# Attention and MLP kernel on one core: every engine in written order, k summed ahead of its product, v pooled by halving adds

## The chip, the cores and the metric

The kernel runs on one core of a Trainium2 chip. The metric is the device time of one launch in microseconds (us); the kernel before takes 438.38 us (median of 3 runs, 438.37 to 439.07). Engines: PE (TensorE, matrix products), DVE (VectorE), ACT (ScalarE), POOL (GpSimd) and SP (SyncE, which here only issues DMAs).

## The reference

Two layers follow each other for 8 batches of 576 tokens and 8 heads of width 64. First an attention whose keys and values are means over 8 tokens (72 of each per head), then a mixing of tokens and a two-layer MLP (512 to 2048 to 512):

```python
k_p = k.reshape(B, H, 72, 8, D).mean(axis=3); v_p = v.reshape(B, H, 72, 8, D).mean(axis=3)
attn = softmax(q @ k_p.T / 8);  x = (attn @ v_p), heads side by side      # B, 576, 512
u = x + lam * einsum('ts,bsd->btd', w_tok, alpha1 * x + beta1)
out = u + lam * (relu((alpha2 * u + beta2) @ w_ch1) @ w_ch2)
```

## The kernel before, in words

Heads are taken in pairs (hp 0 to 3). For a batch b and a pair, `load_qk` (L72) loads q and k as 128 partitions of four tokens each, and the last 64 tokens by further DMAs; `load_v` (L94) loads v, 72 groups of 8 tokens. All these DMAs are issued by SP. `cast_qk` (L84) makes bf16 of q and k, four instructions a pair, on POOL in the main loop. `att_F` (L227) transposes q on PE (L233, L235), copies it to `qT` (L240, ACT), pools k by four products with a 0/1 matrix and one for the last 64 tokens (L245, L247), and casts the result to `kpT` (L249, L250, DVE). `att_V` (L252) pools v on DVE: one reduction over 8 tokens for each head (L256). `att_S` (L260) makes scores and their exponentials (ACT, L269) of one head; `att_AV` (L273) the product with v, whose quotient goes to x (DVE, L288, L290). `att_X` (L293) makes xs, the scaled x, for a range of heads (DVE, L297, L301). `mix_T` (L317) is the token mixing of one chunk of 128 tokens: five products on PE (L324), then u and u_bf on DVE (L327, L329). `mix_uT` (L332) transposes u_bf on PE (L340) and copies it by ACT (L342). Four chunks make a block of 512 tokens; there are 9 blocks. `mlp_A` (L348) is the first layer for one of 16 slices (four products, L351; ReLU by ACT, L354), `mlp_B` (L359) a quarter of the second layer for one of four chunks (L364), whose last quarter ends with an add on DVE (L369) and a store by SP.

The loop at L434 writes block n's 16 `mlp_A` and 16 `mlp_B` together with the attention of batch n+1 and the loads of batch n+2. Each step has a due time, in units of one `mlp_A`, and they are written in the order of due times: `att_F` of pair hp at 1.5 + 3.5 hp, `att_V` at 2 + 3.5 hp, the scores from 14.5, `att_AV` from 16.6, `att_X` at 20.7, 22.7 and 24.7, `mix_T` from 26, `mix_uT` from 27.8. Block 0 also holds three `setup_bias` (L217, PE) and four `scale_w2` (L210, DVE, due 8.2, 10.2, 12.2, 14.2). Blocks 7 and 8 have no attention.

Written order is not what runs: the framework orders each engine's instructions itself, by its own estimate of when each is ready, and an engine then runs its list strictly in order. Ahead of the loop, L378 to L410 write batch 0's attention, the load of the weights w1 and w2 (POOL's DMAs, cast on the way), the transposes of w_tok (`setup_wtok`, L172), the loads of batch 1 and the first four `mix_T`.

Of the kernel before, what the change touches and what calls it, by code (L numbers as in the profile page):

```python
# [23 lines left out]
def kernel(  # L24
# [98 lines left out]

    def bcast(src, name):
        t = const.tile([P, DM], FP, tag=name, name=name)
        nc.scalar.dma_start(out=t, in_=src.unsqueeze(0).to_broadcast((P, DM)))
        return t

    lam_bc = bcast(moe_lam, "lam_bc")
    al1_bc = bcast(moe_alpha1, "al1_bc")  # L130
    b1_bc = bcast(moe_beta1, "b1_bc")
    al2_bc = bcast(moe_alpha2, "al2_bc")
    b2col = const.tile([P, 4], FP, tag="b2col", name="b2col")
    nc.scalar.dma_start(out=b2col, in_=moe_beta2.rearrange("(c p) -> p c", p=P))


# [350 lines left out]
```

## Time and profile before

| | us |
|---|---|
| median of 3 runs | 438.38 |
| the profiled execution | 437.62 |
| its span on the core | 435.9 |
| PE busy / DVE busy / ACT busy / POOL busy | 370.4 / 233.2 / 181.8 / 71.9 |
| first product of the MLP (block 0 begins) | 64.46 |
| last add | 430.94 to 431.63 |

In the rows further down a timeline line gives start, duration, engine, line, operation, output and inputs, their shape and the count, and in brackets the idle time ahead of it with what ended that. A product's duration includes its way through the array, so that the distance of two starts, not the duration, is its cost. PEclk is the granted share of PE's clock.

### The profile page before, as it was taken

What the parts mean: (1) busy time and instruction counts of PE and PEld (TensorE: products, weight loads), DVE (VectorE), ACT (ScalarE), POOL (GpSimd) and SP (SyncE); (2) the same over time, 40 slices, a digit from 0 to 9 for tenths busy, and PEclk for the clock granted to TensorE, in tenths of its full rate; (3) what the DMA queues carried; (4) which work ended last, traced back from release to release, by engine and by line L of the source; (5) the groups of instructions that cost most, each with busy time, mean ns of one, the idle gap of its engine ahead of it and who ended that gap; (6) DMA issues with size and microseconds to landing.
All of it is one profiled execution on the core that took longest, in us unless ns stands there. A gap on an engine that the chain in (4) does not pass through costs nothing.

```text
span 435.9 us, 6112 instructions
## 1 busy us (share of the span) xinstructions
PE 370.4 (85%) x2315; PEld 191.5 (44%) x2358; DVE 233.2 (53%) x484; ACT 181.8 (42%) x348; POOL 71.9 (17%) x139
## 2 busy tenths in 40 slices
PE   0266529997899899978998999789989999999995
PEld 0145214553455345534553455345534554444442
DVE  3688479299318941894179417950696158301011
ACT  1133115741575057504760576047604771560720
POOL 2541629600140014001400140002000000000000
...
GB/s 206 227 257 224 251 210 131 227 226 134 43 145 132 104 50 141 130 104 25 164 117 117 28 110 76 102 28 2 16 59 24 2 26 48 26 0 72 26 24 72
DMA packets 43436, 44.71 MB, mean 103 GB/s; under 512 B 12624, under 2 KB 33104, under 8 KB 43408
## 3 DMA queue, kind: packets, MB, share of 16 engines
...
q10 hardware_dynamic: 1104, 1.05, 0.9%
q8 instruction: 18, 0.29, 0.3%
q14 instruction: 10, 0.08, 0.1%
...
## 4 chain that ended last, share of the span: by engine, by line
PE 55%; DVE 29%; DMA 12%; issue 2%; SPq 1%; ACT 0%
PE ps_h L351 29%; PE ps_ch L364 11%; DVE vp L256 10%; PE ps_tok L324 6%; DMA qk_raw<-in_q_dram 6%; DVE x_tm L290 5%; DVE xs L297 4%; DVE u_sb L369 4%; DMA v_hp<-in_v_dram 3%; PE ps_uT L340 2%; DMA b2col<-in_moe_beta_dram 2%; DVE u_sb L327 2%; DVE u_bf L329 2%; DVE rec L288 1%; PE ps_q L233 1%
## 5 line engine op out<-in xcount | busy, mean ns | idle before, releaser
L364 PE MATMUL ps_ch<-w,Hj 128*128 128x512 bf16 x553 | 136.5, 379 | 1.7 <-issue 0.6
L351 PE MATMUL ps_h<-u_fm,w 128*128 128x512 bf16 x557 | 132.1, 381 | 1.8 <-ACT u_fm L342 0.7
L354 ACT ACTIVATE Hj<-ps_h,bias_cols 128x512 bf16<-128x512 f32 x144 | 98.9, 687 | 57.0 <-PE ps_h L351 54.0
L351 PEld LDWEIGHTS <-w 128*128 128x128 bf16 x576 | 53.7, 98 | 59.9 <-issue 1.8
L89 POOL CAST qk_bf<-qk_raw 128x512 bf16<-128x512 f32 x60 | 42.5, 709 | 224.3 <-issue 153.4
L342 ACT COPY u_fm<-ps_uT 128x512 bf16<-128x512 bf16 x36 | 21.1, 585 | 130.8 <-PE ps_uT L340 130.8
L364 PEld LDWEIGHTS <-Hj 128*128 128x128 bf16 x576 | 51.8, 98 | 52.0 <-issue 1.6
L256 DVE TENSOR_REDUCE vp<-v_hp 72x64 f16<-72x512 f32 x64 | 63.3, 1002 | 7.4 <-DMA v_hp<-in_v_dram 7.2
L324 PE MATMUL ps_tok<-xs,wtT 128*128 128x512 bf16 (+2 forms) x199 | 50.6, 391 | 10.4 <-DVE xs L297 10.2
L269 ACT ACTIVATE ET<-ps_sc 72x288 f16<-72x288 f32 x128 | 43.9, 407 | 31.6 <-PE ps_sc L267 31.4
L369 DVE TENSOR_TENSOR u_sb<-u_sb,ps_ch 128x512 f32<-128x512 f32 x36 | 24.5, 681 | 51.4 <-PE ps_ch L364 48.3
L249 DVE CAST kpT<-ps_kp 64x72 bf16<-64x72 f32 x32 | 7.1, 223 | 81.0 <-PE ps_kp L247 80.9
L267 PE MATMUL ps_sc<-qT,kpT 128*72 128x288 bf16 x128 | 27.6, 307 | 9.7 <-DVE kpT L249 9.7
L327 DVE TENSOR_TENSOR u_sb<-x_tm,ps_tok 128x512 f32<-128x512 f32 (+1 forms) x40 | 26.8, 681 | 14.4 <-PE ps_tok L324 14.4
L324 PEld LDWEIGHTS <-wtT 128*128 128x128 bf16 (+3 forms) x200 | 19.2, 103 | 33.7 <-issue 17.6
L340 PE MATMUL ps_uT<-identity_bf,u_bf 128*128 128x128 bf16 x144 | 14.6, 226 | 20.7 <-DVE u_bf L329 20.7
L290 DVE TENSOR_TENSOR x_tm<-ps_av,rec 128x320 f32<-128x320 f32 x64 | 29.9, 480 | 0.3
L329 DVE TENSOR_TENSOR u_bf<-u_sb,al_bc 128x512 bf16<-128x512 f32 (+1 forms) x40 | 27.7, 705 | 0.8
L288 DVE RECIPROCAL rec<-ps_av 128x5 f32<-128x5 f32 x64 | 11.1, 182 | 30.4 <-PE ps_av L286 30.2
L91 POOL CAST qk_bf<-qk_raw 64x128 bf16<-64x128 f32 x60 | 25.7, 429 | 2.2 <-DMA qk_raw<-in_k_dram 1.8
L267 PEld LDWEIGHTS <-kpT 128*72 128x72 bf16 x128 | 14.9, 119 | 22.9 <-DVE kpT L249 10.0
L340 PEld LDWEIGHTS <-u_bf 128*128 128x128 bf16 x144 | 9.5, 99 | 33.1 <-DVE u_bf L329 29.8
...
## 6 DMA issues: line engine op xcount, KB each, us to landing
...
```

The lines of the kernel that those rows point to most:

```text
L89: eng.tensor_copy(out=bf[:, i, 0:4].rearrange("p c h d -> p h c d"), in_=raw[:, i, :, 0:4, :])
L256: nc.vector.tensor_reduce(out=vp1_pool[hp][:, hh, 0:64], in_=v_hp[:, hh].rearrange("g p d -> g d p"), axis=AX.X, op=ALU.add)
L267: nc.tensor.matmul(out=ps_sc[0:SPG, 0:288], lhsT=kpT_pool[hp][:, hh, :], rhs=st["qT"][hp][:, n0:n0 + 288])
L269: nc.scalar.activation(out=ET[:, n0:n0 + 288], in_=ps_sc[0:SPG, 0:288], func=AF.Exp, bias=0.0, scale=0.125)
L290: nc.vector.tensor_tensor(out=x[:, :, dd:dd + D], in0=av[:, :, 0:64], in1=rec.unsqueeze(2).to_broadcast((P, 5, D)), op=ALU.mult)
L324: nc.tensor.matmul(out=ps_tok[p0:p1, 0:DM], lhsT=wtT[0:kk, at, P * c:P * c + (p1 - p0)], rhs=xs[0:kk, sc, :], start=(sc == 0), stop=(sc == 4))
L327: nc.vector.tensor_tensor(out=s["u"][p0:p1, :], in0=st1[b]["x"][p0:p1, c, :], in1=ps_tok[p0:p1, 0:DM], op=ALU.add)
L329: nc.vector.tensor_tensor(out=s["u_bf"][p0:p1, :], in0=s["u"][p0:p1, :], in1=al2_bc[p0:p1, :], op=ALU.mult)
L351: nc.tensor.matmul(out=ps_h, lhsT=w1[:, cc, P * j:P * j + P], rhs=u_fm[n][:, cc, :], start=(cc == 0), stop=(cc == 3))
L354: nc.scalar.activation(out=t, in_=ps_h, func=AF.Relu, bias=bias_cols[:, j:j + 1], scale=1.0)
L364: nc.tensor.matmul(out=ps, lhsT=Hj[n, j][:, 128 * m:128 * m + 128], rhs=w2[:, j, :], start=(j == 0), stop=(j == NJ - 1))
L369: nc.vector.tensor_tensor(out=u, in0=u, in1=ps, op=ALU.add)
```

## The change

Every engine runs its instructions in the order in which they are written (`manual_schedule`). q and k of the last 64 tokens come for all heads at once (`load_rem`) and are cast by one instruction. q is cast by itself, k is not cast: POOL sums its four tokens per partition by two adds (`sum_k`), the second of which writes bf16, so that `att_F` has one product with the pooling matrix in place of four. `att_V` sums 8 tokens by three adds on DVE, both heads at once, in place of two reductions. `qT` has 4 buffers in place of 3. Ahead of the loop the loads of batch 0 are put in another order, with w_tok and two vectors among them; w_tok is loaded in whole rows, cast to bf16 by two DVE instructions and transposed in bf16; its row sums come from ten products with ones (`setup_rowsum`); POOL issues the parts of w1 between the adds of batch 0 (512, 512 and 1024 columns), then w2. The due times in the loop stay, but for the new steps.

```diff
     nc = tc.nc
+    ctx.enter_context(tc.manual_schedule())
...
     def load_qk(b, hp):
-        raw = work.tile([P, 2, 2, 5, D], FP, tag="qk_raw", bufs=4, name="qk_raw")
+        raw = work.tile([P, 2, 2, 4, D], FP, tag="qk_raw", bufs=4, name="qk_raw")
         for i, src in enumerate((q, k)):
-            two = src[b, 2 * hp:2 * hp + 2]
             nc.sync.dma_start(
-                out=raw[:, i, :, 0:4, :].rearrange("p h c d -> p h (c d)"),
-                in_=two[:, 0:512, :].rearrange("h (p c) d -> p h (c d)", c=4))
-            nc.sync.dma_start(out=raw[0:REM, i, :, 4, :],
-                              in_=two[:, 512:576, :].rearrange("h p d -> p h d"))
+                out=raw[:, i].rearrange("p h c d -> p h (c d)"),
+                in_=src[b, 2 * hp:2 * hp + 2, 0:512, :].rearrange("h (p c) d -> p h (c d)", c=4))
         st1[b]["raw"][hp] = raw
-    def cast_qk(b, hp, engines):
-        raw = st1[b]["raw"][hp]
-        bf = work.tile([P, 2, 5, 2, D], BF, tag="qk_bf", bufs=6, name="qk_bf")
-        for i, eng in enumerate(engines):
-            eng.tensor_copy(out=bf[:, i, 0:4].rearrange("p c h d -> p h c d"),
-                            in_=raw[:, i, :, 0:4, :])
-            eng.tensor_copy(out=bf[0:REM, i, 4], in_=raw[0:REM, i, :, 4, :])
-        st1[b]["bf"][hp] = bf
+    def load_rem(b):
+        raw = work.tile([REM, 2, H, D], FP, tag="rem_raw", bufs=2, name="rem_raw")
+        for i, src in enumerate((q, k)):
+            nc.sync.dma_start(out=raw[:, i], in_=src[b, :, 512:576, :].rearrange("h p d -> p h d"))
+        st1[b]["rem_raw"] = raw
...
+    def cast_rem(b, eng):
+        bf = work.tile([REM, 2, H, D], BF, tag="rem_bf", bufs=2, name="rem_bf")
+        eng.tensor_copy(out=bf, in_=st1[b]["rem_raw"])
+        st1[b]["rem"] = bf
+    def cast_q(b, hp, copy):
+        bf = work.tile([P, 4, 2, D], BF, tag="q_bf", bufs=5, name="q_bf")
+        copy(out=bf.rearrange("p c h d -> p h c d"), in_=st1[b]["raw"][hp][:, 0])
+        st1[b]["q"][hp] = bf
+    def sum_k(b, hp, eng):
+        raw = st1[b]["raw"][hp][:, 1]
+        bf = work.tile([P, 2, D], BF, tag="k_bf", bufs=5, name="k_bf")
+        eng.tensor_tensor(out=raw[:, :, 0:2], in0=raw[:, :, 0:2], in1=raw[:, :, 2:4], op=ALU.add)
+        eng.tensor_tensor(out=bf, in0=raw[:, :, 0], in1=raw[:, :, 1], op=ALU.add)
+        st1[b]["k"][hp] = bf
...
+    def cast_wtok(eng):
+        eng.tensor_copy(out=wt_bf[:, 0:4], in_=wt_sb[:, 0:4])
+        eng.tensor_copy(out=wt_bf[0:REM, 4], in_=wt_sb[0:REM, 4])
+    def load_wtok():
+        nc.sync.dma_start(out=wt_sb[:, 0:4, :],
+                          in_=moe_w_tok[0:512, :].rearrange("(p c) s -> p c s", c=4))
+        nc.sync.dma_start(out=wt_sb[0:REM, 4, :], in_=moe_w_tok[512:576, :])
...
     new_batch(0)
-    for hp in range(4):
-        load_v(0, hp)
-        load_qk(0, hp)
+    load_qk(0, 0)
+    load_rem(0)
+    load_v(0, 0)
+    load_qk(0, 1)
+    load_v(0, 1)
+    load_vec(lam_bc, moe_lam)
+    load_vec(lamal_bc, moe_alpha1)
+    load_qk(0, 2)
+    load_wtok()
+    load_v(0, 2)
+    load_qk(0, 3)
+    load_v(0, 3)
+    load_vec(al2_bc, moe_alpha2)
...
     def setup_vectors():
+        nc.vector.tensor_tensor(out=lamal_bc, in0=lamal_bc, in1=lam_bc, op=ALU.mult)
+        for i, p0 in ((0, 64), (1, 0)):
+            nc.vector.tensor_tensor(out=xs_pool[i][p0:p0 + 1, 4, :], in0=b1row[p0:p0 + 1, :],
+                                    in1=lam_bc[p0:p0 + 1, :], op=ALU.mult)
+        ps = gp("ps_vec")
+        nc.tensor.transpose(out=ps[:, 0:4], in_=b2row, identity=identity[0:4, 0:4])
+        nc.vector.tensor_copy(out=b2c_bf, in_=ps[:, 0:4])
     def setup_wtok(tcx):
         trc = P if tcx < 4 else REM
+        w = wt_bf[0:trc, tcx, :]
         strided = w[:, 0:512].rearrange("p (m c) -> p c m", c=4)
+        ps_w = gp("ps_w").bitcast(BF)
         for sc in range(4):
+            nc.tensor.transpose(out=ps_w[0:P, trc * sc:trc * sc + trc], in_=strided[:, sc, :],
+                                identity=identity_bf[0:trc, 0:trc])
+        nc.tensor.transpose(out=ps_w[0:64, 4 * trc:5 * trc], in_=w[:, 512:576],
+                            identity=identity_bf[0:trc, 0:trc])
+        nc.tensor.transpose(out=ps_w[0:P, 5 * trc:6 * trc], in_=w[:, 448:576],
+                            identity=identity_bf[0:trc, 0:trc])
         cols = slice(P * tcx, P * tcx + trc)
         nc.scalar.copy(out=wtT[:, 0:4, cols],
+                       in_=ps_w[:, 0:4 * trc].rearrange("p (s t) -> p s t", t=trc))
+        nc.vector.tensor_copy(out=wtT[0:64, 4, cols], in_=ps_w[0:64, 4 * trc:5 * trc])
+        nc.vector.tensor_copy(out=wtT[64:128, 5, cols], in_=ps_w[64:128, 5 * trc:6 * trc])
+    def setup_rowsum():
+        for half in range(2):
+            cols = slice(288 * half, 288 * half + 288)
+            ps = gp("ps_rs")
+            for sc in range(5):
+                kk = P if sc < 4 else REM
+                nc.tensor.matmul(out=ps[:, 0:288], lhsT=ones_bf[0:kk, :],
+                                 rhs=wtT[0:kk, sc, cols], start=(sc == 0), stop=(sc == 4))
+            nc.vector.tensor_copy(out=wtT[64:65, 4, cols], in_=ps[64:65, 0:288])
+            nc.vector.tensor_copy(out=wtT[0:1, 5, cols], in_=ps[0:1, 0:288])
...
     def att_F(b, hp):
         st = st1[b]
-        qT = work.tile([P, S], BF, tag="qT", bufs=3, name="qT")
+        qT = work.tile([P, S], BF, tag="qT", bufs=4, name="qT")
         ps_q = gp("ps_q").bitcast(BF)
+        rem_q = st["rem"][:, 0, 2 * hp:2 * hp + 2, :].rearrange("p h d -> p (h d)")
+        rem_k = st["rem"][:, 1, 2 * hp:2 * hp + 2, :].rearrange("p h d -> p (h d)")
         for c in range(4):
             nc.tensor.transpose(out=ps_q[0:P, 128 * c:128 * c + 128],
+                                in_=st["q"][hp][:, c].rearrange("p h d -> p (h d)"),
+                                identity=identity_bf)
+        nc.tensor.transpose(out=ps_q[0:P, 512:576], in_=rem_q, identity=identity_bf[0:REM, 0:REM])
+        nc.scalar.copy(out=qT, in_=ps_q[:, 0:S])
         st["qT"][hp] = qT
         kpT = kpT_pool[hp]
         ps_kp = gp("ps_kp")
-        for c in range(4):
-            nc.tensor.matmul(out=ps_kp[0:P, 0:64], lhsT=bf[:, 1, c],
-                             rhs=pool_main, start=(c == 0), stop=(c == 3))
-        nc.tensor.matmul(out=ps_kp[0:P, 64:72], lhsT=bf[0:REM, 1, 4],
-                         rhs=pool_rem)
+        nc.tensor.matmul(out=ps_kp[0:P, 0:64], lhsT=st["k"][hp].rearrange("p h d -> p (h d)"),
+                         rhs=pool_main)
+        nc.tensor.matmul(out=ps_kp[0:P, 64:72], lhsT=rem_k, rhs=pool_rem)
         nc.vector.tensor_copy(out=kpT[0:64, 0, :], in_=ps_kp[0:64, 0:SPG])
         nc.vector.tensor_copy(out=kpT[64:128, 1, :], in_=ps_kp[64:128, 0:SPG])
     def att_V(b, hp):
-        v_hp = st1[b]["v"][hp]
-        with nc.allow_low_precision(reason="fp16 AV keeps fp32 accumulation in PSUM"):
-            for hh in range(2):
-                nc.vector.tensor_reduce(out=vp1_pool[hp][:, hh, 0:64],
-                                        in_=v_hp[:, hh].rearrange("g p d -> g d p"),
-                                        axis=AX.X, op=ALU.add)
+        t = st1[b]["v"][hp]
+        for n in (4, 2):
+            nc.vector.tensor_tensor(out=t[:, :, 0:n], in0=t[:, :, 0:n], in1=t[:, :, n:2 * n],
+                                    op=ALU.add)
+        nc.vector.tensor_tensor(out=vp1_pool[hp][:, :, 0:64], in0=t[:, :, 0], in1=t[:, :, 1],
+                                op=ALU.add)
...
+    def pro_in(hp):
+        cast_q(0, hp, nc.scalar.copy)
+        if hp == 0:
+            cast_rem(0, nc.gpsimd)
+        sum_k(0, hp, nc.gpsimd)
+        att_F(0, hp)
+        att_V(0, hp)
+    def pro_S(hp):
+        att_S(0, 2 * hp)
+        att_S(0, 2 * hp + 1)
+    def pro_AV(hp):
+        att_AV(0, 2 * hp)
+        att_AV(0, 2 * hp + 1)
+    new_batch(1)
+    pro_in(0)
+    pro_S(0)
+    pro_in(1)
     setup_vectors()
+    load_w1(0, 512)
+    pro_AV(0)
+    pro_S(1)
+    pro_in(2)
+    load_w1(512, 1024)
+    pro_AV(1)
+    att_X(0, 0, 4)
+    pro_S(2)
+    cast_wtok(nc.vector)
+    pro_in(3)
+    load_w1(1024, 2048)
+    setup_wtok(0)
+    setup_wtok(1)
+    pro_AV(2)
+    pro_S(3)
+    setup_wtok(2)
+    setup_wtok(3)
+    setup_wtok(4)
+    setup_rowsum()
+    pro_AV(3)
+    att_X(0, 4, 8)
     for hp in range(4):
         load_qk(1, hp)
...
+        if hp == 0:
+            load_rem(1)
         load_v(1, hp)
     for g in range(4):
         load_w2(g)
...
-        todo = []
+        todo = [(-2.0, lambda: cast_rem(b, nc.gpsimd))]
         for hp in range(4):
-            todo.append((-1.0 + 3.5 * hp, lambda hp=hp: cast_qk(b, hp, (nc.gpsimd, nc.gpsimd))))
+            todo.append((-1.0 + 3.5 * hp,
+                         lambda hp=hp: cast_q(b, hp, nc.gpsimd.tensor_copy)))
+            todo.append((-0.9 + 3.5 * hp, lambda hp=hp: sum_k(b, hp, nc.gpsimd)))
             todo.append((1.5 + 3.5 * hp, lambda hp=hp: att_F(b, hp)))
             todo.append((2.0 + 3.5 * hp, lambda hp=hp: att_V(b, hp)))
...
                 new_batch(b + 1)
+                todo.append((3.5, lambda b=b: load_rem(b + 1)))
                 for hp in range(4):
                     todo.append((3.6 + 3.5 * hp, lambda b=b, hp=hp: load_v(b + 1, hp)))
                     todo.append((3.7 + 3.5 * hp, lambda b=b, hp=hp: load_qk(b + 1, hp)))
```

## Rows read from the trace of the kernel before

**Rows 1.** Busy time by stretch, one per block of the loop: 0, 1, 2, 6.

```profile
core 0: us, PE busy (x) PEld busy (x) DVE busy (x) ACT busy (x) POOL busy (x), PEclk, DMA share, GB/s
64.46:113.60 49.14, 44.49 (x314) 22.98 (x321) 37.31 (x60) 20.78 (x43) 18.73 (x24) 0.97 0.59 165
113.60:156.70 43.10, 40.74 (x264) 21.03 (x267) 24.25 (x51) 21.21 (x41) 6.56 (x16) 1.00 0.34 107
156.70:202.18 45.48, 41.10 (x266) 21.19 (x269) 26.97 (x54) 20.63 (x40) 6.56 (x16) 1.00 0.35 103
...
333.77:375.50 41.73, 40.72 (x266) 21.23 (x270) 20.41 (x46) 20.63 (x40) 0.00 (x0) 1.00 0.08 26
```

**Rows 2.** Timeline of PE, block 3: first and last pieces of its second half.

```profile
219.66 1.03 PE L364 MATMUL ps_ch<-w,Hj 128*128 128x512 bf16 x4
...
234.98 2.33 PE L324 MATMUL ps_tok<-xs,wtT 128*128 128x512 bf16 x10 [1.44 <-DVE xs L297]
```

**Rows 3.** Timeline of DVE, block 3, ahead of the token mixing and in it.

```profile
221.35 1.03 DVE L256 TENSOR_REDUCE vp<-v_hp 72x64 f16<-72x512 f32 x1
...
233.33 0.99 DVE L256 TENSOR_REDUCE vp<-v_hp 72x64 f16<-72x512 f32 x1
234.25 0.67 DVE L297 TENSOR_TENSOR xs<-x_tm,lamal_bc 128x512 bf16<-128x512 f32 x1
...
235.65 1.95 DVE L256 TENSOR_REDUCE vp<-v_hp 72x64 f16<-72x512 f32 x2
```

**Rows 4.** Timeline of PE, block 6, where no v of a later batch is pooled.

```profile
351.26 1.03 PE L364 MATMUL ps_ch<-w,Hj 128*128 128x512 bf16 x4
...
363.95 1.24 PE L324 MATMUL ps_tok<-xs,wtT 128*128 128x512 bf16 x5 [0.32 <-DVE xs L297]
...
375.25 0.40 PE L340 MATMUL ps_uT<-identity_bf,u_bf 128*128 128x128 bf16 x4 [0.32 <-DVE u_bf L329]
```

**Rows 5.** Timeline of all engines, ahead of block 0: DVE, PE.

```profile
43.39 2.27 DVE L211 TENSOR_TENSOR w<-w,lam_bc 128x2048 bf16<-128x2048 bf16 x1
43.51 0.61 PE L324 MATMUL ps_tok<-xs,wtT 128*128 128x512 bf16 x1
...
56.94 1.93 DVE L256 TENSOR_REDUCE vp<-v_hp 72x64 f16<-72x512 f32 x2 [7.18 <-DMA v_hp<-in_v_dram]
...
59.38 1.00 DVE L256 TENSOR_REDUCE vp<-v_hp 72x64 f16<-72x512 f32 x1
...
61.50 1.02 DVE L256 TENSOR_REDUCE vp<-v_hp 72x64 f16<-72x512 f32 x1
...
64.46 0.59 PE L351 MATMUL ps_h<-u_fm,w 128*128 128x512 bf16 x1 [0.67 <-ACT u_fm L342]
```

**Rows 6.** Timeline of PE, block 3: one att_F, q's transposes to the next mlp_A.

```profile
203.91 0.39 PE L233 MATMUL ps_q<-identity_bf,qk_bf 128*128 128x128 bf16 x4
...
204.36 0.29 PE L245 MATMUL ps_kp<-pool_main,qk_bf 128*128 128x64 bf16 x4
204.59 0.18 PE L247 MATMUL ps_kp<-pool_rem,qk_bf 64*128 64x8 bf16 x1
204.69 3.63 PE L351 MATMUL ps_h<-u_fm,w 128*128 128x512 bf16 x16
```

**Rows 7.** Timeline of DVE, block 3: two-input instructions of 512, 256 and 128 elements.

```profile
229.18 0.41 DVE L301 TENSOR_TENSOR xs<-x_tm,lamal_bc 64x256 bf16<-64x256 f32 x1
...
230.53 0.68 DVE L297 TENSOR_TENSOR xs<-x_tm,lamal_bc 128x512 bf16<-128x512 f32 x1
231.13 0.28 DVE L301 TENSOR_TENSOR xs<-x_tm,lamal_bc 64x128 bf16<-64x128 f32 x1
```

**Rows 8.** Timeline of POOL, block 3: casts of 512 and 128 elements.

```profile
204.89 0.61 POOL L89 CAST qk_bf<-qk_raw 128x512 bf16<-128x512 f32 x1 [31.89 <-issue]
205.44 0.29 POOL L91 CAST qk_bf<-qk_raw 64x128 bf16<-64x128 f32 x1
```

**Rows 9.** Busy time by stretch of 5 us, columns as in rows 1.

```profile
5.00:10.00 5.00, 0.61 (x4) 0.34 (x4) 1.94 (x3) 1.28 (x1) 0.00 (x0) 1.00 1.08 273
...
15.00:20.00 5.00, 0.99 (x5) 0.71 (x6) 4.91 (x11) 0.49 (x2) 2.85 (x4) 1.00 1.00 232
```

**Rows 10.** Timelines of POOL and DVE, block 0: a cast beside scale_w2.

```profile
73.30 4.08 POOL L91 CAST qk_bf<-qk_raw 64x128 bf16<-64x128 f32 x1
...
74.95 2.27 DVE L211 TENSOR_TENSOR w<-w,lam_bc 128x2048 bf16<-128x2048 bf16 x1
```

More of the change, by code (lines that the diff above doesn't have):

```diff
@@ new lines, with load_vec @@
+    b2row = const.tile([4, P], FP, tag="b2row", name="b2row")
+    def load_vec(t, src):
+        nc.sync.dma_start(out=t, in_=src.unsqueeze(0).to_broadcast((t.shape[0], DM)))
+    nc.scalar.dma_start(out=b2row, in_=moe_beta2.rearrange("(c p) -> c p", p=P))
+    for p0 in (0, 64):
+        nc.scalar.dma_start(out=b1row[p0:p0 + 1, :], in_=moe_beta1.unsqueeze(0))
+    new_batch(0)
+    load_qk(0, 0)
[4 more added lines that the diff above has]
+    load_vec(lam_bc, moe_lam)
@@ L122 @@
                             fill=1.0, base=0, pattern=[[-1, P]], channel_multiplier=1)
[L124 to L134, printed above, removed]
-    wt_sb = const.tile([P, 5, 641], FP, tag="wt_sb", name="wt_sb")
-    for s0, s1, at in ((0, 512, 0), (512, 576, 576)):
-        nc.sync.dma_start(out=wt_sb[:, 0:4, at:at + s1 - s0],
-                          in_=moe_w_tok[0:512, s0:s1].rearrange("(p c) s -> p c s", c=4))
-        nc.sync.dma_start(out=wt_sb[0:REM, 4, at:at + s1 - s0], in_=moe_w_tok[512:576, s0:s1])
+    nc.vector.memset(ones_bf, 1.0)
     vp1_pool, kpT_pool, ET_pool = [], [], []
@@ L172, in setup_wtok @@
+        nc.vector.tensor_copy(out=b2c_bf, in_=ps[:, 0:4])
     def setup_wtok(tcx):
         trc = P if tcx < 4 else REM
-        w = wt_sb[0:trc, tcx, :]
-        part = work.tile([P, 2], FP, tag="wsum", bufs=2, name="wsum")
-        nc.vector.tensor_reduce(out=part[0:trc, 0:1], in_=w[:, 0:512], axis=AX.X, op=ALU.add)
-        nc.vector.tensor_reduce(out=part[0:trc, 1:2], in_=w[:, 576:640], axis=AX.X, op=ALU.add)
-        for at in (512, 640):
-            nc.vector.tensor_tensor(out=w[:, at:at + 1], in0=part[0:trc, 0:1],
-                                    in1=part[0:trc, 1:2], op=ALU.add)
+        w = wt_bf[0:trc, tcx, :]
@@ L228, in att_F @@
         st = st1[b]
-        bf = st["bf"][hp].rearrange("p i c h d -> p i c (h d)")
-        qT = work.tile([P, S], BF, tag="qT", bufs=3, name="qT")
+        qT = work.tile([P, S], BF, tag="qT", bufs=4, name="qT")
         ps_q = gp("ps_q").bitcast(BF)
+        rem_q = st["rem"][:, 0, 2 * hp:2 * hp + 2, :].rearrange("p h d -> p (h d)")
+        rem_k = st["rem"][:, 1, 2 * hp:2 * hp + 2, :].rearrange("p h d -> p (h d)")
         for c in range(4):
             nc.tensor.transpose(out=ps_q[0:P, 128 * c:128 * c + 128],
-                                in_=bf[:, 0, c], identity=identity_bf)
-        nc.tensor.transpose(out=ps_q[0:P, 512:576], in_=bf[0:REM, 0, 4],
-                            identity=identity_bf[0:REM, 0:REM])
-        if b == 0 and hp % 2:
-            nc.vector.tensor_copy(out=qT, in_=ps_q[:, 0:S])
-        else:
-            nc.scalar.copy(out=qT, in_=ps_q[:, 0:S])
+                                in_=st["q"][hp][:, c].rearrange("p h d -> p (h d)"),
+                                identity=identity_bf)
+        nc.tensor.transpose(out=ps_q[0:P, 512:576], in_=rem_q, identity=identity_bf[0:REM, 0:REM])
+        nc.scalar.copy(out=qT, in_=ps_q[:, 0:S])
         st["qT"][hp] = qT
@@ L375, in mlp_B @@
                     nc.sync.dma_start(out=out[b + i, 512:576, :], in_=u[64 * i:64 * i + 64, :])
-    for hp in range(4):
-        cast_qk(0, hp, (nc.vector, nc.gpsimd))
-    for g in range(4):
-        load_w1(g)
-    setup_vectors()
-    new_batch(1)
+    def pro_in(hp):
[15 more added lines that the diff above has]
+    pro_in(1)
+    setup_vectors()
+    load_w1(0, 512)
[19 more added lines that the diff above has]
+    att_X(0, 4, 8)
     for hp in range(4):
         load_qk(1, hp)
-    for hp in range(4):
-        att_V(0, hp)
-        att_F(0, hp)
-        att_S(0, 2 * hp)
-        att_S(0, 2 * hp + 1)
-        if hp:
-            att_AV(0, 2 * hp - 2)
-            att_AV(0, 2 * hp - 1)
-        if hp == 2:
-            att_X(0, 0, 4)
-    for hp in range(4):
+        if hp == 0:
+            load_rem(1)
         load_v(1, hp)
@@ L399 @@
         load_w2(g)
-    att_AV(0, 6)
-    att_AV(0, 7)
-    for tcx in range(5):
-        setup_wtok(tcx)
-    att_X(0, 4, 8)
     for c in range(4):
```

38 lines of the change are left out of this document (13 added, 25 removed).

## The prediction, made before the change was run

> **What bounds the kernel now.** I read first the busy time by stretch, cut where each block's first MLP product starts. PE is busy for 40.7 to 41.1 us in every block that holds an attention, yet the blocks last 43.10, 45.48 and 41.73 us [rows 1]; blocks 3 and 5 are within 0.02 us of block 1, and block 4 (45.39) is near block 2. So PE is the bound, with 2.4 to 4.4 us of waiting a block, and block 6 almost none. Next, PE's timeline of a block: the first half runs without a gap, and the gap stands ahead of the token mixing, 1.44 us, ended by DVE's last xs [rows 2]. Then DVE's timeline of the same stretch: from 221 to 237 us DVE is never idle, and among its work stand reductions over v, two at a time for each pair of heads [rows 3]. They are att_V of the batch after: the framework has pulled them ahead, between a reciprocal and its quotient, six of the eight ahead of the last xs. Written, they are due in the next block's first half, where DVE does little. Block 6 is the same program without those eight, and its mixing starts 363.95 - 351.26 = 12.69 us after the first piece of the MLP's second layer, against 234.98 - 219.66 = 15.32 us [rows 2, 4].
>
> Ahead of block 0 the order costs more. Batch 0's mixing starts at 43.51 us and the MLP at 64.46 us, 20.95 us later, for four mixings and four transposes. DVE stands for 7.18 us before a reduction over v of batch 1, which has not landed, while u of batch 0 waits behind it; four reductions of batch 1 (1.93 + 1.00 + 1.02) and one scale_w2 (2.27) run there too [rows 5].
>
> **Part by part.** Every sum is made against the profiled execution, 437.62 us, of which 435.9 is the span; the median of the runs is 438.38, 0.76 above, and I add that at the end. A measurement of this kernel can tell about 0.2% from no change.
>
> *The blocks, order and v.* In written order att_V goes to the first half. Its cost there: three adds of 512, 256 and 128 elements a partition. Instructions with two inputs of these sizes took 0.68, 0.41 and 0.28 us [rows 7], so 1.4 us a pair against two reductions of about 1.0 [rows 3]; 5.5 us a batch, beside 219.66 - 202.18 = 17.5 us of PE's first half [rows 1, 2] where DVE has only eight casts to kpT. Their cover is that half; were it gone, they would cost what the reductions cost now. Behind each att_V wait only the casts to kpT of the next pair, due 3.5 units later. Block 6 shows what the second half is worth without v: its PE order is, but for single MLP products moved into gaps, the order of the due times, and it still has two waits of 0.32 us for DVE [rows 4].
>
> *The blocks, k.* Four products with the pooling matrix start at 204.36 and the one for the rest at 204.59, so 0.0575 us each; three of four go, 0.17 a pair and 0.69 us a batch, on the path, since PE has no gap there [rows 6]. The whole att_F takes 204.69 - 203.91 = 0.78 us.
>
> So a block with an odd batch (2, 4, 6, which have a fifth transpose and its wait) becomes 41.73 - 0.69 = 41.0, and one with an even batch (1, 3, 5), without that transpose (0.23, four small products as k's) and that wait (0.32), 40.4. Before, the six sum to 261.9; after, 3 x 41.0 + 3 x 40.4 = 244.2: **17.7 us less**. The bounds: 4.1 (only the products go) and 20.
>
> *POOL.* Per pair, casts of 512 elements took 0.61 and of 128 took 0.29 [rows 8], hence 0.4 for 256 on that line. POOL now has a cast of q (0.61), adds of 256 and 128 elements and, once a batch, a cast of 1024 (about 1.0, on that line). No row shows an add on POOL: the lower bound is the cast, 0.69 us for both adds, the upper a cast held up beside scale_w2, 4.08 us for one instruction [rows 10]. I take 1.2 us, near the casts, since two inputs should take up to twice as long: 8.2 us a batch in a block of 41, a whole block ahead of need. The cover is the buffers: five of q and k let POOL work on batch b+1 as soon as att_F of b lets one go. The Trainium skill (GPSIMD Engine Reference, section 3.1) has 4.5 us for an add of 2048 elements, 2.2 ns an element; by that the two adds would take about 0.85 us, an estimate, and no sum here would change by more than 0.4.
>
> *SP, ACT, qT.* SP issues 14 loads a batch in place of 20, none behind a store that is late, as the loads come at 3.5 to 14.2 and the stores at 19 to 31. ACT has no new work in the blocks. A fourth qT takes away a wait of its copy. All at nothing.
>
> *Ahead of block 0.* By shapes, SP's loads up to the last pair's k are 5.1 MB and POOL's first two parts of w1 1.05 MB. The DMA moved 273 GB/s at best and 232 in a usual stretch early on [rows 9]: 6.15 MB at 232 is 26.5 us, and with 3 us for the start all is there at about 30 us (bounds: 22 us, without w1 at the better rate, and 34). From there the chain is written in order: cast and adds of the last pair, att_F, the scores, w_tok's transposes and row sums, two att_AV, att_X; by the DVE work in it (att_V 1.4, twelve small casts of about 0.25, four quotients 2.6, att_X 1.6) and the PE work between, which comes one after the other, 12 to 14 us. So the mixing starts at about 43 us, **as before**: what the cast of w_tok and fewer DVE instructions save, later loads and the row sums take. What does go is behind it: 7.18 + 1.93 + 1.00 + 1.02 + 2.27 = 13.4 of the 20.95 us [rows 5]. 20.95 - 13.4 leaves 7.5 us; I take 9, since the four mixings then wait for each other's adds on DVE and for the bias products of block 0. The MLP starts at 52, **12.4 us earlier** (bounds: 3, if loads are late by 9, and 17).
>
> *Block 0.* It is 49.14 us [rows 1]: an odd block with 3.7 us more (a mixing, three setup_bias, a slow start). By the odd blocks' new time 41.0 + 3.7 = 44.7. But now all four scale_w2 (2.27 each, 9.1 us) fall on DVE between due times 8.2 and 16, together with att_V of two pairs (2.8) and kpT (0.9), where PE takes some 10.3 us (8 mlp_A at 0.87, from four of them in 3.5 us [rows 6], two att_F, three scores): DVE enters the second half 2.5 us late, and I leave 2.0 on the path, as a block's DVE has little slack until the mixing. 46.7 us: **2.4 us less** (bounds: 0 and 5).
>
> *The end.* Blocks 7 and 8 and the last store are the same: 0.
>
> Sum: 17.7 + 12.4 + 2.4 = 32.5; 437.62 - 32.5 = 405.1, on the median's footing **406 us**.
>
> **Rivals.** *(a) The due order has its own waits.* PE runs strictly as written, and whatever DVE or ACT is late with holds all behind it; now the framework fills gaps with MLP products. Then the blocks keep their 2.4 to 4.4 us and give only 4.1: 406 + 13.6 = 420 us. Against it, block 6, where almost nothing is filled in [rows 4]; for it, that fillers stand there at all. Chance 0.12.
>
> *(b) The loads bound the start.* w1's last 1024 columns and w2 are issued only after POOL's adds of the last pair, at 31 us or later, and compete with batch 1. Then the MLP starts or stalls as late as before: 406 + 12.4 = 418 us. For it: the DMA already moves 232 to 273 GB/s early on [rows 9], so that nothing lands sooner for being asked sooner. Against: the data to be there by the middle of block 0 are 13.4 MB, at 232 GB/s 61 us with the start, and that is when block 0 needs its last parts. Chance 0.13.
>
> *(c) POOL becomes the bound: slower.* Beside scale_w2 a cast of POOL took 4.08 us in place of 0.29, and it ended with that instruction of DVE [rows 8, 10]. The new att_V has two inputs in SBUF as scale_w2 has, and runs where POOL works. POOL has 13 instructions a batch: at a mean of 4.0 us that is 52 us against 40.7, and six blocks give 406 + 68 = 474 us; it decides from 3.5 us, where the blocks cost what is gained elsewhere. The Trainium skill (SBUF - State Buffer, "Who interferes with whom") has the rule: a DVE instruction with two SBUF inputs and a POOL instruction that reads SBUF shut each other out for the whole instruction, and a reduction on DVE does not. That speaks against this change, and the trace's 4.08 us agrees with the lock. Against the size: DVE's own instruction lasts 2.27 us there and at most 0.68 in att_V, so a wait should be that long. Chance 0.07.
>
> *(d) The order is not what is written*, because the framework still moves v up. Then only v's smaller cost counts (six reductions in the tail become 1.8 us shorter) and k's 0.69, some 15 us in six blocks, and nothing is won at the start: 421 us. Chance 0.05.
>
> **How the numbers follow.** The forecast has 0.63, (a) 0.12, (b) 0.13, (c) 0.07, (d) 0.05. The forecast's own bounds are 394 (blocks 20, start 17, block 0 5, and a little more POOL or DVE room) and 415; (a), (b) and (d) lie at 418 to 421, so the range is 394 to 423; outside are (c) and the tails, about 0.15. All but (c) are faster; I keep 0.02 for (a) and (b) together with more lost: faster 0.91, same 0.02, slower 0.07.
>
> **What would show it.** Right: in the blocks, att_V's adds stand between kpT's casts in the first half; DVE's second half holds none; the mixing starts some 12.7 us after the first piece of the second layer; odd blocks last 41.0, even 40.4; att_F costs 0.61. The MLP starts near 52 us and DVE has no wait of 7 us before it. Wrong: a gap of PE over 1 us in each block ahead of a transpose or a mixing (a); an MLP start past 58 us, or waits on w1 or w2 in block 0 (b); POOL's adds above 3 us, with PE waiting for q or k (c); adds of v in the second half (d).

## The result, and the profile after

The changed kernel takes **410.51 us** (median of 4 runs, 409.3 to 410.8) against 438.68 us for the kernel before, beside it on the same chip: ratio 0.9352, 95% interval [0.933, 0.9374]. Run again with the last experiments it took 409.33 us, ratio 0.934 [0.9291, 0.9389]. The profiled execution took 409.3 us, its span is 407.2.

Busy time by stretch, cut as in [rows 1]; the stretches are blocks 0, 1, 2 and 6:

```profile
core 0: us, PE busy (x) PEld busy (x) DVE busy (x) ACT busy (x) POOL busy (x), PEclk, DMA share, GB/s
52.98:99.39 46.41, 43.38 (x310) 22.48 (x310) 36.82 (x62) 20.81 (x43) 18.67 (x15) 1.00 0.38 106
99.39:140.13 40.74, 40.35 (x256) 20.73 (x254) 24.56 (x56) 21.24 (x41) 8.46 (x13) 1.00 0.37 114
140.13:182.03 41.90, 40.73 (x259) 20.86 (x258) 26.25 (x58) 20.66 (x40) 8.09 (x13) 1.00 0.37 110
305.40:347.29 41.89, 40.72 (x258) 20.82 (x257) 26.14 (x58) 20.66 (x40) 0.00 (x0) 1.00 0.08 26
```

Blocks 1 to 6 sum to 347.29 - 99.39 = 247.9 us, 13.9 less than before, and block 0 lost 2.8. PE now waits 0.39 us in block 1 and 1.17 in block 2. The rest came ahead of block 0. PE's timeline: the start, then block 0's two waits over 1 us, block 2 (an odd batch) and block 3 (an even one):

```profile
42.96 4.45 PE L358 MATMUL ps_tok<-xs,wtT 128*128 128x512 bf16 x10 [2.86 <-DVE xs L331]
...
52.98 1.02 PE L385 MATMUL ps_h<-u_fm,w 128*128 128x512 bf16 x4 [0.67 <-ACT u_fm L376]
...
78.06 1.02 PE L398 MATMUL ps_ch<-w,Hj 128*128 128x512 bf16 x4 [1.51 <-DVE w L248]
...
87.84 1.25 PE L358 MATMUL ps_tok<-xs,wtT 128*128 128x512 bf16 x5 [1.21 <-DVE xs L331]
...
170.47 1.25 PE L358 MATMUL ps_tok<-xs,wtT 128*128 128x512 bf16 x5 [0.85 <-DVE xs L331]
181.79 0.40 PE L374 MATMUL ps_uT<-identity_bf,u_bf 128*128 128x128 bf16 x4 [0.32 <-DVE u_bf L363]
...
199.16 1.03 PE L398 MATMUL ps_ch<-w,Hj 128*128 128x512 bf16 x4
...
211.91 1.25 PE L358 MATMUL ps_tok<-xs,wtT 128*128 128x512 bf16 x5 [0.39 <-DVE xs L331]
```

The mixing begins at 42.96 us, as in [rows 5]; the MLP begins at 52.98 in place of 64.46. The 1.44 us of [rows 2] is 0.39 in an even block, and 0.85 in an odd one.

One att_F on PE, against [rows 6], then v's adds between the casts to kpT on DVE in the first half:

```profile
141.86 0.39 PE L271 MATMUL ps_q<-identity_bf,q_bf 128*128 128x128 bf16 x4
142.18 0.20 PE L274 MATMUL ps_q<-identity_bf,rem_bf 64*128 64x64 bf16 x1
142.31 0.20 PE L279 MATMUL ps_kp<-pool_main,k_bf 128*128 128x64 bf16 x1
142.45 0.18 PE L281 MATMUL ps_kp<-pool_rem,rem_bf 64*128 64x8 bf16 x1
142.56 3.63 PE L385 MATMUL ps_h<-u_fm,w 128*128 128x512 bf16 x16
```

```profile
142.90 0.24 DVE L283 CAST kpT<-ps_kp 64x72 bf16<-64x72 f32 x1
143.16 1.14 DVE L289 TENSOR_TENSOR v_hp<-v_hp 72x512 f32<-72x512 f32 x2
144.34 0.29 DVE L291 TENSOR_TENSOR vp<-v_hp 72x128 f16<-72x128 f32 x1
146.82 0.23 DVE L282 CAST kpT<-ps_kp 64x72 bf16<-64x72 f32 x1 [2.19 <-PE ps_kp L281]
```

POOL's adds of k, alone and (first row) beside a scale_w2:

```profile
63.45 2.96 POOL L110 TENSOR_TENSOR qk_raw<-qk_raw 128x256 f32<-128x256 f32 x1
...
149.27 0.72 POOL L110 TENSOR_TENSOR qk_raw<-qk_raw 128x256 f32<-128x256 f32 x1
150.07 0.46 POOL L111 TENSOR_TENSOR k_bf<-qk_raw 128x128 bf16<-128x128 f32 x1
```

### The profile page after: what moved, and what is told of

The parts are those of the page before. It is cut to its first block, busy times and chain, and to the rows that moved or that the text cites. A ratio compares the mean times of both kernels' runs of the same rounds, so it can differ in the third digit from the quotient of the medians.

```text
span 407.2 us, 5942 instructions
## 1 busy us (share of the span) xinstructions
PE 369.7 (91%) x2273; PEld 187.2 (46%) x2273; DVE 226.9 (56%) x493; ACT 185.6 (46%) x354; POOL 81.5 (20%) x117
## 4 chain that ended last, share of the span: by engine, by line
PE 72%; DVE 18%; DMA 5%; SPq 1%; issue 1%; POOL 1%; ACT 0%; ACTq 0%
PE ps_h L385 29%; PE ps_ch L398 20%; PE ps_tok L358 12%; DVE xs L331 4%; DVE x_tm L324 4%; DMA qk_raw<-in_k_dram 3%; PE ps_sc L301 3%; DVE w L248 2%; PE ps_uT L374 2%; DMA lam_bc<-in_moe_lam_dram 2%; DVE u_sb L403 1%; PE ps_q L271 1%; DVE rec L322 1%; DVE xs L335 1%; PE ps_av L316 1%; DVE v_hp L289 1%
## 5 line engine op out<-in xcount | busy, mean ns | idle before, releaser
L398 PE MATMUL ps_ch<-w,Hj 128*128 128x512 bf16 x576 | 140.6, 379 | 1.5 <-DVE w L248 1.5
L358 PE MATMUL ps_tok<-xs,wtT 128*128 128x512 bf16 (+3 forms) x200 | 52.0, 393 | 7.8 <-DVE xs L331 7.8
L289 DVE TENSOR_TENSOR v_hp<-v_hp 72x512 f32<-72x512 f32 x64 | 36.5, 571 | 6.2 <-DMA v_hp<-in_v_dram 4.1
L97 POOL CAST rem_bf<-rem_raw 64x1024 bf16<-64x1024 f32 x8 | 8.2, 1031 | 125.0 <-DMA rem_raw<-in_k_dram 101.0
L324 DVE TENSOR_TENSOR x_tm<-ps_av,rec 128x320 f32<-128x320 f32 x64 | 31.5, 492 | 2.2
L110 POOL TENSOR_TENSOR qk_raw<-qk_raw 128x256 f32<-128x256 f32 x32 | 26.0, 812 | 25.7 <-DMA qk_raw<-in_k_dram 22.7
L103 POOL CAST q_bf<-qk_raw 128x512 bf16<-128x512 f32 x28 | 19.8, 708 | 52.8 <-DMA qk_raw<-in_q_dram 39.5
L322 DVE RECIPROCAL rec<-ps_av 128x5 f32<-128x5 f32 x64 | 12.1, 190 | 23.4 <-PE ps_av L320 23.2
L271 PE MATMUL ps_q<-identity_bf,q_bf 128*128 128x128 bf16 x128 | 13.3, 230 | 12.1 <-ACT q_bf L103 12.1
L275 ACT COPY qT<-ps_q 128x576 bf16<-128x576 bf16 x32 | 20.2, 632 | 6.0 <-PE ps_q L274 6.0
```

The lines of the kernel that those rows point to most:

```text
L110: eng.tensor_tensor(out=raw[:, :, 0:2], in0=raw[:, :, 0:2], in1=raw[:, :, 2:4], op=ALU.add)
L289: nc.vector.tensor_tensor(out=t[:, :, 0:n], in0=t[:, :, 0:n], in1=t[:, :, n:2 * n], op=ALU.add)
L324: nc.vector.tensor_tensor(out=x[:, :, dd:dd + D], in0=av[:, :, 0:64], in1=rec.unsqueeze(2).to_broadcast((P, 5, D)), op=ALU.mult)
L358: nc.tensor.matmul(out=ps_tok[p0:p1, 0:DM], lhsT=wtT[0:kk, at, P * c:P * c + (p1 - p0)], rhs=xs[0:kk, sc, :], start=(sc == 0), stop=(sc == 4))
L398: nc.tensor.matmul(out=ps, lhsT=Hj[n, j][:, 128 * m:128 * m + 128], rhs=w2[:, j, :], start=(j == 0), stop=(j == NJ - 1))
```

## The experiments

Twelve runs; from each trace I read where the MLP starts, block 0, and blocks 1 to 6 together (us):

| kernel | us | ratio to before | MLP start | block 0 | blocks 1 to 6 |
|---|---|---|---|---|---|
| before | 438.68 | 1 | 64.46 | 49.20 | 261.8 |
| order_only | 426.47 | 0.9739 [0.9709, 0.9768] | 65.99 | 48.69 | 250.0 |
| edits_only | 422.22 | 0.9615 [0.957, 0.966] | 64.36 | 45.69 | 246.5 |
| order_casts | 418.88 | 0.9561 [0.9535, 0.9587] | 58.94 | 47.13 | 250.1 |
| after | 410.51 | 0.9352 [0.933, 0.9374] | 52.98 | 46.41 | 247.9 |
| after_again | 409.33 | 0.934 [0.9291, 0.9389] | 51.73 | 46.49 | 247.9 |
| late_wtok | 409.06 | 0.9344 [0.9294, 0.9394] | 51.60 | 47.14 | 247.9 |
| v_reduce | 408.68 | 0.934 [0.9315, 0.9364] | 52.48 | 47.94 | 248.0 |
| k_products | 409.95 | 0.9364 [0.9341, 0.9388] | 51.34 | 47.65 | 250.0 |
| loads_plain | 407.80 | 0.9311 [0.9278, 0.9344] | 50.46 | 48.14 | 247.9 |
| scale_early | 406.82 | 0.9293 [0.9266, 0.9319] | 51.77 | 46.29 | 247.9 |
| rem_last | 403.78 | 0.9205 [0.9174, 0.9236] | 51.87 | 47.14 | 243.4 |
| combo | 398.08 | 0.9087 [0.9059, 0.9114] | 51.17 | 42.66 | 241.7 |
| combo_plain | 399.82 | 0.9119 [0.9078, 0.916] | 52.60 | 44.25 | 241.7 |

In written order, blocks 1 to 6 repeat within 0.1 us where nothing in them was changed; the start and block 0 vary by 1 to 2 us. A median alone can't settle a part worth less than that. The parts of *edits_only* are those of its fastest execution, 418.43 us, 3.8 below its median; in which part the others lose isn't known.

### The order and the other edits, apart

*order_only*: the kernel before, in written order.

```diff
+    ctx.enter_context(tc.manual_schedule())
-        qT = work.tile([P, S], BF, tag="qT", bufs=3, name="qT")
+        qT = work.tile([P, S], BF, tag="qT", bufs=4, name="qT")
```

> The kernel before, every engine in written order, and qT with 4 buffers; no other edit of the change. My theory (the order pays, because v is pooled in the first half of its own block and no longer ahead of the token mixing): blocks 1 to 6 last 41.4 and 42.6 us in turn (those of the changed kernel and 0.7 us for the three products of k), no reduction of v in a second half, DVE's reductions of 2 us a pair hidden; the start is hardly better (MLP at 60 to 64 us), since the loads and the steps ahead of block 0 are the old ones. Time 418 to 430, likeliest 424. Rival (the cheaper instructions pay, the order does not): the blocks stay at 43 to 45 us and the time is 432 or more.

*edits_only*: the changed kernel, ordered by the framework.

```diff
-    ctx.enter_context(tc.manual_schedule())
```

> The changed kernel without the written order: the framework orders each engine itself, all other edits stay. My theory: the adds of v are pulled ahead into the second half again, and blocks 1 to 6 go back by 1.5 to 3 us each; MLP start 53 to 62 us; time 418 to 432, likeliest 424. Rival (the cheaper instructions pay): 412 or less, blocks as in the changed kernel.

Both times came as expected, but the parts did not. In the blocks either half is a cure by itself: the order alone gives 11.8 us, the edits alone 15.3 (at least 11.5, if the 3.8 us were lost there), both 13.9. In *edits_only* the framework still pulls v's adds into the second half (DVE's timeline, block 3):

```profile
212.28 0.20 DVE L321 RECIPROCAL rec<-ps_av 128x5 f32<-128x5 f32 x1 [0.54 <-PE ps_av L319]
212.40 0.25 DVE L290 TENSOR_TENSOR vp<-v_hp 72x128 f16<-72x128 f32 x1
212.56 0.48 DVE L323 TENSOR_TENSOR x_tm<-ps_av,rec 128x320 f32<-128x320 f32 x1
```

The 0.25 us add stands where a reduction of 1.0 us stood [rows 3]; ahead of this block's last xs there are five adds of 1.85 us in all, where six reductions took 6.0. This block lasts 40.45 us and block 2 41.96. That the size of the pieces is why is argued: reductions in the framework's order, with the other edits, weren't run.

At the start neither half gives anything: 65.99 and 64.36 us against 64.46, and 52 together. In *edits_only* the mixing starts at 49.22, and DVE still takes batch 1's v ahead of batch 0's u:

```profile
51.31 0.69 DVE L288 TENSOR_TENSOR v_hp<-v_hp 72x512 f32<-72x512 f32 x1 [1.06 <-DMA v_hp<-in_v_dram]
...
54.66 1.28 DVE L360 TENSOR_TENSOR u_sb<-x_tm,ps_tok 128x512 f32<-128x512 f32 x2
```

*order_only* shows the opposite fault: DVE's timeline, its cast of the last pair's q ahead of the first v, then the first of five rounds through w_tok, then PE:

```profile
20.07 0.43 DVE L90 CAST qk_bf<-qk_raw 128x512 bf16<-128x512 f32 x1 [3.20 <-DMA qk_raw<-in_q_dram]
...
23.38 1.91 DVE L257 TENSOR_REDUCE vp<-v_hp 72x64 f16<-72x512 f32 x2
...
44.08 0.68 DVE L177 TENSOR_REDUCE wsum<-wt_sb 128x1 f32<-128x512 f32 x1
...
46.03 0.29 DVE L195 CAST wtT<-ps_wb 65x128 bf16<-65x128 f32 x1 [0.78 <-PE ps_wb L193]
...
55.21 1.21 DVE L298 TENSOR_TENSOR xs<-x_tm,lamal_bc 128x1024 bf16<-128x1024 f32 x1
```

```profile
56.47 3.96 PE L325 MATMUL ps_tok<-xs,wtT 128*128 128x512 bf16 x10 [1.58 <-DVE xs L298]
...
65.99 1.28 PE L352 MATMUL ps_h<-u_fm,w 128*128 128x512 bf16 x4 [0.67 <-ACT u_fm L343]
```

The mixing starts 13.0 us later than before, and the MLP then only 9.5 us after it, where it was 20.95. The written order does take away the waits of [rows 5], and gives all of it back ahead of the mixing.

*order_casts* adds to *order_only* the place of the first batch's casts, and with it that of the vectors' set-up, of w1's loads and of batch 1's loads of q and k:

```diff
+    new_batch(1)
     for hp in range(4):
         cast_qk(0, hp, (nc.vector, nc.gpsimd))
-    for g in range(4):
-        load_w1(g)
-    setup_vectors()
-    new_batch(1)
-    for hp in range(4):
-        load_qk(1, hp)
-    for hp in range(4):
+        if hp == 1:
+            setup_vectors()
+        if hp == 3:
+            for g in range(4):
+                load_w1(g)
+            for h2 in range(4):
+                load_qk(1, h2)
         att_V(0, hp)
```

> The written order alone (426.5 us) with one more part of the change: each pair of the first batch is cast just ahead of its own heads, where there all four casts stand ahead of the first. If DVE's wait for the last pair's q (to 20 us) is what made the start of that run late, the first heads start at 13 us, the mixing at 47 to 49 in place of 56, and the time is 417 to 420 us. If the loads' landing sets it anyway, or the chain through w_tok, the time stays above 424 us.

The first theory held: the mixing starts at 48.93 us and the MLP 7.05 us earlier. The run does not part the casts from what moves with them. From 58.94 to the 51.7 to 53.0 of the changed kernel 6 to 7.2 us are left. *late_wtok* asks whether they are due to the place of w_tok's transposes:

```diff
-    setup_wtok(0)
-    setup_wtok(1)
     pro_AV(2)
     pro_S(3)
-    setup_wtok(2)
...
+    pro_AV(3)
+    for tcx in range(5):
+        setup_wtok(tcx)
     setup_rowsum()
-    pro_AV(3)
```

> The changed kernel with the five transposes of w_tok and its row sums behind the last pair's quotients, where the kernel before has them, in place of between the heads. If their place is what keeps the mixing at 43 us although the order is now written, PE, ACT and DVE work one after the other through them with nothing to fill the waits: the mixing starts 3 to 5 us later, at 46 us, and the time is 413 to 415 us. If the shorter rewrite alone keeps it, the time stays within 1 us of the changed kernel's.

The place is not the reason: with w_tok last, the mixing starts at 41.39 us, as in *after_again* (41.34). DVE's timeline from the last quotient to xs:

```profile
33.52 0.49 DVE L324 TENSOR_TENSOR x_tm<-ps_av,rec 128x320 f32<-128x320 f32 x1
33.93 0.21 DVE L220 COPY wtT<-ps_w 64x128 bf16<-64x128 bf16 x1
...
39.75 0.45 DVE L233 CAST wtT<-ps_rs 1x288 bf16<-1x288 f32 x1
40.13 1.20 DVE L331 TENSOR_TENSOR xs<-x_tm,lamal_bc 128x1024 bf16<-128x1024 f32 x1
```

What is shorter is the chain: 40.13 - 33.93 = 6.2 us from the first copy to xs, against 55.21 - 44.08 = 11.1 in *order_only* (11.0 in *order_casts*), where each round reduces, transposes and copies in turn. Here the cast of w_tok is done before, and PE transposes while DVE still makes quotients. That the rewrite is worth these 4.9 of the 6 to 7.2 us is argued: no run has it alone, and the rest is not taken apart.

*loads_plain* undoes the order of the first loads (v, q and k of all four pairs, then the vectors, then w_tok):

```diff
+    for hp in range(4):
+        load_v(0, hp)
+        load_qk(0, hp)
...
+    load_vec(al2_bc, moe_alpha2)
     load_wtok()
```

> The changed kernel with SP's first loads in a plain order: v, q, k of all four pairs, the last 64 tokens behind the first pair, then the vectors, then w_tok. My theory (the start is bound by the steps behind the last landing, and w_tok is needed only after the last pair's q and k): the last pair lands some 6 us earlier and w_tok about 4 us later, so the mixing starts within 2 us of 43: 408 to 413. Rival (the order of the loads is what won the start): MLP 6 us or more later, 416 or more.

POOL's add of the last pair's k, in the changed kernel, then here:

```profile
27.18 0.71 POOL L110 TENSOR_TENSOR qk_raw<-qk_raw 128x256 f32<-128x256 f32 x1 [8.92 <-DMA qk_raw<-in_k_dram]
```

```profile
16.21 0.71 POOL L110 TENSOR_TENSOR qk_raw<-qk_raw 128x256 f32<-128x256 f32 x1 [0.47 <-DMA qk_raw<-in_k_dram]
```

The last pair's k is there 11 us sooner, but the mixing starts at 40.31 us, only 1.0 ahead of *after_again* and 2.7 ahead of the changed kernel's first run. The MLP starts at 50.46 us, no later, and the time is 407.8: the reordered loads bring nothing that can be seen.

### k and v

*k_products*: POOL casts k, PE makes four products again.

```diff
-        bf = work.tile([P, 2, D], BF, tag="k_bf", bufs=5, name="k_bf")
-        eng.tensor_tensor(out=raw[:, :, 0:2], in0=raw[:, :, 0:2], in1=raw[:, :, 2:4], op=ALU.add)
-        eng.tensor_tensor(out=bf, in0=raw[:, :, 0], in1=raw[:, :, 1], op=ALU.add)
+        bf = work.tile([P, 4, 2, D], BF, tag="k_bf", bufs=3, name="k_bf")
+        eng.tensor_copy(out=bf.rearrange("p c h d -> p h c d"), in_=raw)
...
+        for c in range(4):
+            nc.tensor.matmul(out=ps_kp[0:P, 0:64],
+                             lhsT=st["k"][hp][:, c].rearrange("p h d -> p (h d)"),
+                             rhs=pool_main, start=(c == 0), stop=(c == 3))
```

> The changed kernel with k cast to bf16 by POOL and pooled by four products as before (three buffers for it in place of five). My theory: 0.69 us more of PE a batch on the path, 4.8 us over seven blocks, less about 0.6 us ahead of block 0, where one cast takes the place of two adds: 413.5 to 416. Rival (hidden, PE has room): 410 to 411.

A miss in the time, and the trace shows why. Its att_F on PE:

```profile
142.25 0.29 PE L279 MATMUL ps_kp<-pool_main,k_bf 128*128 128x64 bf16 x4
142.47 0.18 PE L282 MATMUL ps_kp<-pool_rem,rem_bf 64*128 64x8 bf16 x1
142.58 3.63 PE L386 MATMUL ps_h<-u_fm,w 128*128 128x512 bf16 x16
```

Four products and the rest's take 0.33 us from the first start to the next mlp_A, one and the rest's 0.25. So three products cost 0.08 a pair, 0.33 a batch: every block with an attention is 0.35 us longer (41.09 and 42.24), 2.1 us in six, and the start's spread covers that.

*v_reduce*: att_V with the two reductions of before.

```diff
-        for n in (4, 2):
-            nc.vector.tensor_tensor(out=t[:, :, 0:n], in0=t[:, :, 0:n], in1=t[:, :, n:2 * n],
...
+            for hh in range(2):
+                nc.vector.tensor_reduce(out=vp1_pool[hp][:, hh, 0:64],
```

> The changed kernel with v pooled by two reductions a pair as before. My theory: some 0.5 us more of DVE a pair, hidden in the blocks' first halves (blocks 40.7 and 41.9 unchanged); 1 to 2 us more ahead of block 0 and in block 0, where DVE is on the path: 411 to 413. Rival (v's cheaper pooling pays by itself): 17 us more of DVE come on the path in whole or half: 418 or more.

Blocks 1 to 6 differ by 0.1 us in all, and the time is not the 411 to 413 us expected. In written order the first half covers either form (1.97 us for the two reductions, 1.4 for the adds), and the halving adds buy nothing there. What they are worth at the start is less than its spread.

### What is left in the way

*rem_last*: xs of the last 64 tokens in one instruction, after the last xs.

```diff
-        p0 = 64 * (b % 2)
-        nc.vector.tensor_tensor(out=xs[p0:p0 + 64, 4, d0:d1], in0=x[p0:p0 + 64, 4, d0:d1],
-                                in1=lamal_bc[p0:p0 + 64, d0:d1], op=ALU.mult)
+        if h1 == H:
+            p0 = 64 * (b % 2)
+            nc.vector.tensor_tensor(out=xs[p0:p0 + 64, 4, :], in0=x[p0:p0 + 64, 4, :],
+                                    in1=lamal_bc[p0:p0 + 64, :], op=ALU.mult)
```

> The changed kernel, but xs of the last 64 tokens is made for all heads by one instruction after the last xs of the other tokens, in place of three. It tests what the 0.39 and 0.85 us are that PE waits ahead of the mixing in blocks 1 to 6 and 1.2 in block 0. My theory (DVE's chain to the last xs ends the wait, and in odd batches these instructions write partitions 64 to 127 between others that write from 0, and do not overlap with them): both waits go, blocks 40.4 and 41.1, 3 to 5 us less: 405.5 to 407.5. Rival (the wait is for something else, ACT or the order of PE): unchanged, 410 to 411.

Busy time by stretch, blocks 2 and 3:

```profile
139.23:180.13 40.90, 40.59 (x258) 20.84 (x257) 25.63 (x56) 20.63 (x40) 8.14 (x13) 1.00 0.38 113
180.13:220.35 40.22, 40.22 (x256) 20.73 (x254) 24.86 (x54) 21.21 (x41) 8.72 (x13) 1.00 0.36 115
```

Blocks 1 to 6 are 4.5 us shorter: 0.52 in an even block (40.22), 0.99 in an odd one (40.90), and the time is below the expected range. In those blocks no wait is left ahead of the mixing; the 0.31 us in block 2 stand ahead of the fifth transpose.

*scale_early*: scale_w2 at 0.35, 2.1, 5.6 and 9.1.

```diff
-                todo.append((8.2 + 2 * g, lambda g=g: scale_w2(g)))
+                todo.append(((0.35, 2.1, 5.6, 9.1)[g], lambda g=g: scale_w2(g)))
```

> The changed kernel with the four scale_w2 of block 0 due at 0.35, 2.1, 5.6 and 9.1 in place of 8.2 to 14.2. My theory (they make DVE late by 2.7 us in block 0's second half): block 0 lasts 43.7 to 45 in place of 46.4; time 408 to 409. Rival (w2 has not landed by then, and DVE waits for it with kpT behind): 411 to 415.

PE's wait of 1.51 us for w2 is gone from the trace. The granted clock in that execution was 0.57 between 52 and 56 us and cost about as much (last section), so block 0 is no shorter: 46.29 us, a miss. The interval lies below that of the changed kernel's first runs and overlaps that of *after_again*, so a gain in time is likely and not shown.

*combo*: both, with the first xs at 20.55 (ahead of the fifth quotient), the second chunk's add to u later, and an odd batch's fifth transpose in the next block.

```diff
-        todo.append((20.7, lambda: att_X(b, 0, 4)))
+        todo.append((20.55, lambda: att_X(b, 0, 4)))
...
+        todo.append((24.8, lambda: mlp_U(n, 1)))
...
+        if n % 2 == 1:
+            todo.append((0.9, lambda: mix_uT((n - 1, 4))))
```

> rem_last and scale_early together, and: the first xs due at 20.55 (ahead of the fifth head's quotient), the add of the second chunk's u due after the last xs, the transposes of an odd batch's last chunk moved into the next block. My theory: all waits of PE in blocks 1 to 6 but those of the mixing's own adds go, 40.3 and 40.6 a block, and 2 to 3 us in block 0: 402 to 405. Rival (new waits in place of the old, the u's add late for its store or the second chunk's bank): 406 or more.

398.08 us beats both kernels and is below the expected range; block 0 alone gives 3.8 us. Busy time by stretch, blocks 2 and 3: PE is never idle there.

```profile
134.23:174.38 40.15, 40.15 (x254) 20.80 (x253) 25.13 (x55) 20.66 (x40) 9.08 (x13) 1.00 0.39 115
174.38:214.78 40.40, 40.40 (x258) 21.02 (x257) 25.08 (x55) 21.05 (x41) 8.10 (x13) 1.00 0.37 115
```

*combo_plain* is *combo* with the edits of *loads_plain* and *v_reduce*, whose diffs stand above. *after_again* is the changed kernel, unaltered.

> All edits of the combination (398.1 us), and with them v, q and k first in the loads and v pooled by two reductions. If neither the order of the first loads nor the halving adds bring anything, 397 to 399 us; if one of them is worth its theory's 1 to 3 us here, where DVE has less slack, 399 to 402 us.

> The changed kernel once more, beside the last run: 409 to 411 us, the mixing at 41 to 43 us; block 0 lasts 46.4 us if the clock is 1.00 between 52 and 56 us and about 1.5 more if it is near 0.6 there, as in most of the other runs.

*after_again* came as expected. *combo_plain*'s 399.82 us lies where it was expected if one of the two edits were worth something. Its blocks 1 to 6 are those of *combo*, and its block 0 is 1.6 us longer beside a granted clock of 0.65 (last section); the MLP starts 1.4 us later, and the two intervals overlap. So in the blocks neither edit brings anything, and a worth of 1 to 2 us at the start is not excluded here.

## Why the prediction was right, and where not

- **The blocks, order and v**: right in mechanism. v is in the first half, and the mixing starts 211.91 - 199.16 = 12.75 us after the second layer's first piece in block 3, where 12.7 was foretold. What was credited to the order is not the order's alone: the edits alone do as much there (15.3 us), and rival (d) priced that at "some 15 us in six blocks". That figure came out with some luck: it counts 0.69 us a batch for k, where 0.35 came.
- **The blocks, k**: the term that was mis-sized. I took 0.0575 us, the spacing of products in a run of four, for what each removed product gives back. att_F costs 0.70 us, not 0.61, and a batch gains 0.35, not 0.69: 2.0 us of the 3.7 missing in the blocks.
- **The odd blocks' wait**: I carried over block 6's 0.32 us; it is 0.85, and three times 0.53 is the other 1.6 us. In DVE's timeline instructions on partitions 64 and up stretch the row of work (last section), which is what tells an odd block from an even one here, 0.85 from 0.39. Block 6 before had them too; there the first xs stood ahead of the fifth quotient, where it now stands behind it, as written. That this makes the 0.53 is argued: *rem_last* takes the whole wait away with the quotient left in its place.
- **Ahead of block 0**: 52.98 us where 52 was said, in part by luck. Behind the mixing the account held: 52.98 - 42.96 = 10.0 us to the MLP, where 9 was said, and *order_only* has 9.5. The mixing's start was right for the wrong reason. I let the last pair's loads set it, at about 30 us, and costed the start's edits at nothing on balance; in *loads_plain* the last pair's k is there 11 us sooner, and the mixing starts only 1.0 to 2.7 us sooner. "As before" is two large terms that cancel: 13.0 us lost by the order, 13.5 won by the edits. For the start of the MLP the order alone gives -1.5 us; the casts' place, with what moves along, gives 7.05, and what is left, w_tok's rewrite with it, 6 to 7.2.
- **Block 0**: 46.41 us for 46.7. I left 2.0 us for scale_w2; the trace has 1.51 <-DVE w, and *scale_early* takes it away. Beside that, two things cancel: the odd block that I started from is 0.9 us longer than said, and the "slow start" that I kept was not there in this execution. Before, the granted clock was 0.61 in the block's first 3.54 us, by 3.54 x (1 - 0.61) a loss of 1.4 us, half of the 2.8 that the block gained:

```profile
64.46:68.00 3.54, 3.32 (x9) 1.13 (x10) 2.72 (x2) 0.69 (x1) 3.54 (x3) 0.61 1.00 253
```

- **POOL**: 0.72 + 0.46 = 1.18 us for the two adds, as taken (1.2), where the Trainium skill's figure for a large add (GPSIMD Engine Reference, section 3.1) gave an estimate of 0.85; the row decides. Rival (c) is real beside scale_w2, 2.4 to 3.0 us an instruction, but in the blocks PE waits for nothing of POOL's.
- **The end**: 60.41 us of span behind block 7's start before, 59.91 after; 0.5 less, not 0.

In sum 11.5 + 13.9 + 2.8 + 0.5 = 28.7 us of the span, for 32.5.
